# The way back of six groups of features by seven half products instead of eight, and two conversion steps of 24 weights on ScalarE

## The chip, the cores and the metric

The kernel runs on one core of a Trainium2 chip. The metric is the time of one execution in device microseconds; the time before is the median of three runs. A profile of one further execution gives the rows below. The engines are TensorE (PE, with its weight loads as PEld), VectorE (DVE), ScalarE (ACT), GpSimd (POOL) and the queue of SyncE (SP).

## The reference

Three parts, all in float32 as far as the result shows: linear attention with a normalization, a gated feed-forward layer, and a second feed-forward layer with an ELU.

```python
kv = np.einsum('bhsd,bhse->bhde', k, v)          # 4 batches, 8 heads, 576 tokens, 64 wide
out = np.einsum('bhsd,bhde->bhse', q, kv)
x = out / rms(out) * g_norm                       # then 2304 tokens x 512
xn = x / rms(x) * rms_g
g = xn @ w_gate                                   # 512 x 1536
x = (g * sigmoid(g) * (xn @ w_val)) @ w_out       # 1536 x 512
h = x @ w_in                                      # 512 x 2048
out = np.where(h > 0, h, np.exp(np.minimum(h, 0)) - 1) @ w_out2   # 2048 x 512
```

## The kernel before

The weights come as 64-bit floats. `conversion` makes 32-bit floats of a 128x512 tile of them in eight steps: `begin`, `scale`, `shift`, `sign`, `tail`, `add` on VectorE (four of them one-input steps of integers or floats, two with two inputs), then `part` on ScalarE and `rest` on VectorE, which split the value into a high part `h` and a low part `l` that TensorE takes as `fp32r`. Every product of the network is made of three such matmuls: high by high, high by low, low by high.

The 2304 tokens lie in five blocks of columns: block 0 with 256 and blocks 1 to 4 with 512. Blocks (1, 2) and (3, 4) are pairs. The hidden features come in chunks of 128: chunk `f` of the first layer has weights `g`, `v` (in) and `o` (back), 12 of them; the second layer has `i` and `p`, 16 of them. In this text "feature 8" is chunk 8. Two chunks make a group (`groups`), and the way back of a group adds up in PSUM over both chunks; the sum over groups is made in DRAM: ScalarE copies a bank to a buffer (`part`, five of them in the pools `P`), and GpSimd issues a DMA that adds it to `mid` (first layer) or `out` (second).

The hidden layer of a pair already goes by Strassen-Winograd's scheme from feature 2 or 4 on, and in all of the second layer (`paired`, named `('pu', layer, feature, first block)` in the rows): the products are made for halves of the model's width and of the pair's columns, seven instead of eight. The table `PRODUCTS` names for each one the bank (`a`, `b` or `c`), the half of the weight or sum of halves, and that of the input. Bank `a` takes the first, sixth, fifth and third product one on the other; ScalarE copies it after each of the first three (`snap`), and VectorE adds bank `b` or `c` to such a copy (`total`). Sums of weight halves are made by `weight_sums` (steps `w`, then `Sh` and `Sl` as their high and low part).

The way back is plain: `back` adds, for each block and each quarter `e` of the outputs, one step for each feature of the group, which is `back_part`: three matmuls of 512 columns (256 in block 0) onto bank `b`. `split_steps` makes the high and low part of an activation (`act`) on ScalarE and VectorE; then `dump` copies the bank.

What stands where on each engine is set by `Plan`: every step has an engine, a length, a rank and the steps and rooms it waits for; the planner takes the step that can start first, by rank where they tie, and writes the program in that order. Each engine then runs its list in order and waits on semaphores. `W` are 20 rooms for parts of weights, `A` those for parts of activations, `U` for intermediate values, `P` for copies on their way to DRAM.

Of the kernel before, what the change touches and what calls it, by code (L numbers as in the profile page):

```python
# [135 lines left out]
def linear_attention__swiglu__elu_kernel(
# [322 lines left out]
    def weight_sums(one, two, rank, users):  # L459

        def quarters():
            a, b = cw[one], cw[two]
# [107 lines left out]
    def split_steps(ph, f, t, erank, src, after, frees):  # L570
# [4 lines left out]
        def high():  # L575
            w = 2 * W if t else W
            a = res.tile([P, w], F32R, tag=plan.where[key], name=f"act{ph}_{f}_{t}")
            h = a[:, :n]
            acts[ph, f, t] = h, a[:, n:2 * n]
            nc.scalar.activation(h, src(), AF.Copy)  # L580
# [632 lines left out]
```

## Time and profile before

| | |
|---|---|
| median of 3 runs | 863.13 us (862.85 to 863.23) |
| profiled execution, its own time | 863.61 us |
| its span, first to last instruction | 861.6 us |
[...]
| TensorE busy | 849.0 us |
| VectorE busy | 641.4 us |
| ScalarE busy | 511.0 us |
| GpSimd busy | 232.8 us |

A busy time is the union of an engine's instructions; the last part of one can lie beside the start of the next, so distances between starts say more of an engine that never stops than durations do. Matmuls overlap most: they last 0.39 us and start 0.23 us apart. What lies around the span is 2.0 us.

### The profile page before, as it was taken

Reading aid. Unit: us, or ns where it says so; the run is one execution under the profiler, and the core shown is the slowest. Engines: PE = TensorE matmul, PEld = TensorE weight load, DVE = VectorE, ACT = ScalarE, POOL = GpSimd, SP = SyncE. Lnnn points to the kernel's source line nnn. Section 1 sums busy time; section 2 is a strip of 40 time slices with the busy share of each in tenths; the row PEclk is TensorE's granted clock in tenths of the full one; section 3 lists DMA queues with packets and bytes.
Section 4 is the critical chain, followed back from the end, with each engine's and each line's share of the span. In section 5 each row is a group of like instructions: output and inputs, shape, how many; then the busy total and the mean of one; then the engine's idle time right before and its main releaser. Section 6 shows DMA issues by size and latency. Waiting matters only on the chain.

```text
span 861.6 us, 12089 instructions
## 1 busy us (share of the span) xinstructions
PE 849.0 (99%) x4204; PEld 713.8 (83%) x4204; DVE 641.4 (74%) x1217; ACT 511.0 (59%) x979; POOL 232.8 (27%) x260
## 2 busy tenths in 40 slices
PE   7999999999999999999999999999999999999998
PEld 7988788888888888888888778888888888888886
DVE  6899899998736856675788999888675757674364
ACT  2788766445544545444544777777675767676652
POOL 2636523053033123113300000224233333423300
PEclk9999999999999999999999999999999999999999
DMA  9941479399076556727911254588788897868686
GB/s 366 364 154 43 117 157 179 92 181 201 28 121 118 111 106 119 142 69 128 220 50 61 74 184 154 129 175 155 148 154 163 145 153 133 170 110 121 124 230 210
DMA packets 57373, 126.14 MB, mean 146 GB/s; under 512 B 6496, under 2 KB 10080, under 8 KB 57312
## 3 DMA queue, kind: packets, MB, share of 16 engines
q0 software_dynamic: 29952, 51.92, 40.4%
q1 hardware_dynamic: 27360, 73.45, 24.3%
q8 instruction: 33, 0.54, 0.2%
q14 instruction: 28, 0.23, 0.1%
HBM read 59.28 MB, written 66.06 MB: 145 GB/s over the span
## 4 chain that ended last, share of the span: by engine, by line
PE 85%; DVE 7%; DMA 3%; ACT 2%; issue 1%; POOL 1%; SPq 0%; ACTq 0%; POOLq 0%; DVEq 0%
PE b L622 36%; PE hid_v L719 4%; PE hid_g L719 4%; PE hid_i L719 2%; PE po L298 1%; PE kv L262 1%; DMA wacc<-in_kv 1%; DMA wxl<-in_kv 1%; DVE xl L363 1%; POOL ri L318 1%; DVE far L693 1%; DVE act L584 1%; PE ('pu', 0, 9, 1)_a L529 1%; PE ('pu', 0, 11, 1)_a L529 1%; PE ('pu', 0, 4, 1)_a L529 1%
## 5 line engine op out<-in xcount | busy, mean ns | idle before, releaser
L657 ACT ACTIVATE part<-b 128x512 f32<-128x512 f32 (+1 forms) x246 | 138.8, 574 | 85.1 <-PE b L622 61.6
L663 POOL DMA_DIRECT2D out<-part x108 | 95.6, 893 | 304.8 <-ACT part L657 234.7
L622 PE MATMUL b<-act,h_p 128*128 128x512 f32 x512 | 158.5, 390 | 0.3 <-DVE act L584 0.2
L663 POOL DMA_DIRECT2D mid<-part x100 | 89.8, 995 | 234.7 <-ACT part L657 227.1
L622 PE MATMUL b<-act,h_o 128*128 128x512 f32 (+1 forms) x480 | 137.6, 370 | 3.0 <-DVE z L321 1.5
L622 PEld LDWEIGHTS b<-act,h_p 128*128 128x128 f32 x512 | 95.3, 188 | 21.1 <-DVE act L584 0.5
L622 PEld LDWEIGHTS b<-act,h_o 128*128 128x128 f32 x480 | 87.1, 188 | 21.7 <-DVE z L321 2.0
L622 PE MATMUL b<-act,l_p 128*128 128x512 f32 x256 | 99.6, 389 | 0.0
L622 PE MATMUL b<-act,l_o 128*128 128x512 f32 (+1 forms) x240 | 88.3, 368 | 0.0
L622 PEld LDWEIGHTS b<-act,l_p 128*128 128x128 f32 x256 | 48.1, 188 | 10.0
L622 PEld LDWEIGHTS b<-act,l_o 128*128 128x128 f32 x240 | 45.1, 188 | 7.6
L584 DVE TENSOR_TENSOR act<-e,act 128x512 fp32r<-128x512 f32 (+1 forms) x80 | 49.6, 631 | 1.5 <-ACT act L580 1.2
L580 ACT ACTIVATE act<-e 128x512 fp32r<-128x512 f32 (+1 forms) x80 | 45.9, 582 | 4.0 <-DVE e L763 3.8
L760 ACT ACTIVATE e<-e 128x512 f32<-128x512 f32 (+1 forms) x80 | 45.9, 583 | 0.8
L318 POOL TENSOR_TENSOR ri<-ms,nhalf 128x8 f32<-128x8 f32 x18 | 34.4, 1937 | 13.7 <-DVE ms L314 13.7
L719 PE MATMUL hid_g<-xh,h_g 128*128 128x256 f32 (+1 forms) x96 | 32.8, 342 | 0.0
L719 PE MATMUL hid_v<-xh,h_v 128*128 128x256 f32 (+1 forms) x96 | 32.5, 339 | 0.0
L719 PE MATMUL hid_g<-xl,h_g 128*128 128x256 f32 (+1 forms) x96 | 32.3, 337 | 0.0
L719 PE MATMUL hid_v<-xh,l_v 128*128 128x256 f32 (+1 forms) x96 | 32.3, 336 | 0.0
L719 PE MATMUL hid_g<-xh,l_g 128*128 128x256 f32 (+1 forms) x96 | 32.3, 336 | 0.0
L719 PE MATMUL hid_v<-xl,h_v 128*128 128x256 f32 (+1 forms) x96 | 32.3, 336 | 0.0
L693 DVE TENSOR_TENSOR far<-far,b 128x512 f32<-128x512 f32 (+1 forms) x38 | 24.3, 653 | 8.3 <-PE b L622 8.3
(1596 smaller groups left out, 2127.3 us busy)
## 6 DMA issues: line engine op xcount, KB each, us to landing
out<-part POOLq DMA_DIRECT2D x108, 256.0 KB, 5.4
mid<-part POOLq DMA_DIRECT2D x80, 256.0 KB, 6.3
raw_i<-in_w_in SPq DMA_DIRECT2D x16, 512.0 KB, 4.3
raw_p<-in_w_out SPq DMA_DIRECT2D x16, 512.0 KB, 4.7
raw_g<-in_w_gate SPq DMA_DIRECT2D x12, 512.0 KB, 5.5
raw_v<-in_w_val SPq DMA_DIRECT2D x12, 512.0 KB, 5.3
raw_o<-in_w_out SPq DMA_DIRECT2D x12, 512.0 KB, 6.9
out<-part SPq DMA_DIRECT2D x18, 256.0 KB, 2.5
```

Of the source, the lines that this page charges most:

```text
L262: nc.tensor.matmul(kv_acc[b][:, p, :], in_sb[i][r0:r1, p * P:(p + 1) * P], in_sb[i][r0:r1, DM + p * P:DM + (p + 1) * P], start=(i == tiles ...
L298: nc.tensor.matmul(po[r:r1, p * P:(p + 1) * P], qt[:, p, r:r1], kv_sb[b][:, p, :], start=True, stop=True)
L318: nc.gpsimd.tensor_tensor(ri, ms_t.pop(i), nhalf, op=ALU.pow)
L529: nc.tensor.matmul(pbank[unit, b], l[:, sl], r, start=first and c == 0 and i == 0, stop=c == 1 and i == 2, skip_group_check=True,)
L580: nc.scalar.activation(h, src(), AF.Copy)
L584: nc.vector.tensor_tensor(l, src(), h.bitcast(F32), op=ALU.subtract)
L622: nc.tensor.matmul(po, l, r, start=f == fs[0] and i == 0, stop=f == fs[-1] and i == 2)
L657: nc.scalar.activation(x, pbank["b", k, t, e][:, :n], AF.Copy)
L663: nc.gpsimd.dma_start(out=where(ph, t, e), in_=live.pop(key), accum_op=ALU.add)
L693: nc.vector.tensor_tensor(x, x, pbank["b", k, t, e][:, :n], op=ALU.add)
L719: nc.tensor.matmul(pbank[key], l, r, start=c == 0 and i == 0, stop=c == KD - 1 and i == 2)
L760: nc.scalar.activation(live[key], live[key], AF.Exp, scale=-1.0)
```

## The change

For six groups, features 4 to 9 of the first layer and groups 4, 8 and 12 (chunks 4 and 5, 8 and 9, 12 and 13) of the second, the way back of the two pairs goes by seven half products too (`back_halved`, `('pb', group, first block)` in the rows). Block 0 of these groups stays plain. The two chunks of the group are the two halves of the sum; the output weights' two halves and the pair's two blocks are the other two. The steps of a pair: high and low parts of three of the four activations and of four differences that are made in place over the activations (`split`, `less`: seven splits, four differences), 14 products of three matmuls on six banks (`a`, `b`, `c` for each of two column halves), eight copies by ScalarE straight into the `part` buffers, and six totals on VectorE. `weight_sums` makes the sums of the output weights' halves (`Sh_o`, `Sl_o`, `Sh_p`, `Sl_p`). An activation of such a group is no longer split by `split_steps`.

For the 24 weights `g`, `v`, `o` of features 4 to 11, `begin` and `tail` become ScalarE's: `Abs` with the scale 2^-112, and `Copy` with scale and bias; `scale` on VectorE keeps the minimum alone. The rooms of `act` are 12 single ones instead of 6 double ones, four of them also free for `U`. For a halved group both `o` are loaded after all `g` and `v`. In the last group of the first layer, block 0's products wait for the first pair's last ones, and the second pair's for block 0's.

```diff
+BACK_HALVED = [(0, 4), (0, 6), (0, 8), (1, 4), (1, 8), (1, 12)]
+SPARE = [f"{x}{f}" for f in range(4, 12) for x in "gvo"]
...
-        "U0": ["t0", "t1", "t2"], "C0": ["t3", "y0", "ad5"], "A0": AD[:3], "P0": P3[:2] + AD[3:5],
+        "U0": ["t0", "t1", "t2"], "C0": ["t3", "y0", "ad11"], "A0": AD[:6], "P0": P3[:2] + AD[6:8],
...
-        "A": AD, "A1": ["y0", "t3"], "P": P3 + K2, "U": Z4 + ["t2"], "C": ["t0", "t1", "t2"],
+        "A": AD, "A1": ["y0", "t3"], "P": P3 + K2, "U": Z4 + ["t2"] + AD[:7:-1], "C": ["t0", "t1", "t2"],
...
-            nc.vector.tensor_scalar(t["c"], t["high"], 0x7FFFFFFF, None, op0=ALU.bitwise_and)
+            if spare:
+                nc.scalar.activation(t["c"].bitcast(F32), t["high"].bitcast(F32), AF.Abs, scale=2.0**-112)
+            else:
+                nc.vector.tensor_scalar(t["c"], t["high"], 0x7FFFFFFF, None, op0=ALU.bitwise_and)
...
+            if spare:
+                nc.vector.tensor_scalar(cf, cf, INF_FIELD, None, op0=ALU.min)
...
+            if spare:
+                nc.scalar.activation(t["c"], t["low"], AF.Copy, scale=2.0**-29, bias=2.0**23)
...
+        turns = {0: [("b", 0, fs[-1], t_, 3) for t_ in PAIRS[0]], PAIRS[1][0]: [("b", 0, fs[-1], 0, 3)], PAIRS[1][1]: [("b", 0, fs[-1], 0, 3)]} if last and ph == 0 else {}
+        if k in HALVED and t:
+            return
...
+        def split(j, x):
+
+            def high():
+                parts[j] = tuple(place((unit, "s", j, y), F32R) for y in range(2))
+                nc.scalar.activation(parts[j][0], raw(*x), AF.Copy)
+
+            def low():
+                nc.vector.tensor_tensor(parts[j][1], raw(*x), parts[j][0].bitcast(F32), op=ALU.subtract)
...
+        split(11, A11)
+        less(1, A12, A11, A11)
+        split(21, A21)
+        less(3, A22, A12, A12)
+        split(3, A12)
+        split(22, A22)
+        less(2, A22, A11, A22)
+        split(2, A22)
+        less(4, A21, A22, A21)
+        split(1, A11)
+        split(4, A21)
...
+        before = {6: "snap1", 5: "snap2", 3: "snap4", 4: "total4"}
...
+            for i, (l, r) in enumerate(((wh, mh), (wh, ml), (wl, mh))):
+                nc.tensor.matmul(pbank[key], l[:, sl], r, start=first and i == 0, stop=i == 2, skip_group_check=True)
+
+        for o, (m, b, a, x, first) in enumerate(PRODUCTS):
+            for c in range(2):
+                plan.add(
+                    (unit, m, c), "PE", 0.68, rank + o + 0.5 * c, lambda m=m, c=c: product(m, c),
+                    [(unit, "l", x), *wdeps[a]] + ([(unit, before[m], c)] if m in before else []),
+                    [("o", (unit, b, c))] if first else [],
+                )
...
+            for m, j in ((1, 1), (6, 2), (5, 4), (3, 0)):
+                plan.add((unit, f"snap{j}", c), "ACT", AP_, rank, lambda j=j, copy=copy: copy(j), [(unit, m, c)], [("P", keys[j])])
+            for j, b, m in ((1, "b", 2), (4, "c", 7), (2, "c", 4)):
+                plan.add((unit, f"total{j}", c), "DVE", EW, rank, lambda j=j, b=b, total=total: total(j, b), [(unit, f"snap{j}", c), (unit, m, c)])
...
+            if k in HALVED and X:
+                back_halved(k, X, r + 50)
+            elif ph == 0 and k == last_k(0) and X:
```

The order on TensorE, where the way back of features 8 and 9 begins for blocks 1 and 2. Before, its products follow the first ones of feature 9's hidden layer for blocks 3 and 4:

```order
L529 MATMUL ('pu', 0, 9, 3)_b<-xh_945,h_g_3343 128x512
L529 MATMUL ('pu', 0, 9, 3)_b<-xl_946,h_g_3343 128x512
L529 MATMUL ('pu', 0, 9, 3)_b<-xh_945,l_g_3353 128x512
L622 MATMUL b_2_0_3875<-act_8_2_3677,h_o_3404 128x512 x2
L622 MATMUL b_2_0_3875<-act_8_2_3677,l_o_3413 128x512
L622 MATMUL b_1_0_3881<-act_8_1_3664,h_o_3404 128x512 x2
L622 MATMUL b_1_0_3881<-act_8_1_3664,l_o_3413 128x512
L622 MATMUL b_1_0_3881<-act_9_1_3863,h_o_3583 128x512 x2
L622 MATMUL b_1_0_3881<-act_9_1_3863,l_o_3594 128x512
```

Now, at the fifth and third product of the same way back, where `a_3889` and `a_3897` are the two column halves of bank `a`:

```order
L909 MATMUL ('pb', 5, 1)_a_3889<-('pb', 5, 1)_s_0_4006,Sh_o_1_3828 128x512
L909 MATMUL ('pb', 5, 1)_a_3889<-('pb', 5, 1)_s_1_4007,Sh_o_1_3828 128x512
L909 MATMUL ('pb', 5, 1)_a_3889<-('pb', 5, 1)_s_0_4006,Sl_o_1_3837 128x512
L909 MATMUL ('pb', 5, 1)_a_3897<-('pb', 5, 1)_s_0_4006,Sh_o_1_3828 128x512
L909 MATMUL ('pb', 5, 1)_a_3897<-('pb', 5, 1)_s_1_4007,Sh_o_1_3828 128x512
L909 MATMUL ('pb', 5, 1)_a_3897<-('pb', 5, 1)_s_0_4006,Sl_o_1_3837 128x512
L547 MATMUL ('pu', 0, 9, 3)_c<-xh_1137,Sh_g_1_3638 128x512
L547 MATMUL ('pu', 0, 9, 3)_c<-xl_1138,Sh_g_1_3638 128x512
L547 MATMUL ('pu', 0, 9, 3)_c<-xh_1137,Sl_g_1_3646 128x512
L909 MATMUL ('pb', 5, 1)_a_3889<-('pb', 5, 1)_s_0_3947,Sh_o_1_3828 128x512
L909 MATMUL ('pb', 5, 1)_a_3889<-('pb', 5, 1)_s_1_3948,Sh_o_1_3828 128x512
L909 MATMUL ('pb', 5, 1)_a_3889<-('pb', 5, 1)_s_0_3947,Sl_o_1_3837 128x512
```

The plain products stood in one piece, 48 in a row; the half products are spread among those of the hidden layer, and two products stand here between one use of a bank and the next.

The order on VectorE, around the first total of feature 10's hidden layer for blocks 3 and 4, close to the end of the first layer. Before:

```order
L555 TENSOR_TENSOR ('pu', 0, 10, 1)_u_4114<-('pu', 0, 10, 1)_u_4114,('pu', 0, 10, 1)_c 128x512
L422 TENSOR_SCALAR c_i_4259<-raw_i_4156 128x512
L788 TENSOR_TENSOR ('pu', 0, 10, 1)_u_4114<-('pu', 0, 10, 1)_u_4114,('pu', 0, 10, 1)_u_4047 128x512
L739 TENSOR_TENSOR sa_0_4247<-sa_0_4247,hid_v_10_0_4240 128x256
L425 ISA w_i_4269<-w_i_4269,c_i_4259 128x1024
L788 TENSOR_TENSOR ('pu', 0, 10, 1)_u_4233<-('pu', 0, 10, 1)_u_4233,s_10_1_4293 128x512
L584 TENSOR_TENSOR act_10_1_4296<-('pu', 0, 10, 1)_u_4114,act_10_1_4296 128x512
L584 TENSOR_TENSOR act_10_0_4303<-sa_0_4247,act_10_0_4303 128x256
L584 TENSOR_TENSOR act_10_2_4309<-('pu', 0, 10, 1)_u_4233,act_10_2_4309 128x512
L555 TENSOR_TENSOR ('pu', 0, 10, 3)_u_4316<-('pu', 0, 10, 3)_u_4316,('pu', 0, 10, 3)_b 128x512
```

Now:

```order
L763 TENSOR_TENSOR sa_0_4339<-sa_0_4339,hid_v_10_0_4335 128x256
L603 TENSOR_TENSOR act_10_1_1_4392<-('pu', 0, 10, 1)_u_4229,act_10_1_0_4391 128x512
L603 TENSOR_TENSOR act_10_0_0_4397<-sa_0_4339,act_10_0_0_4397 128x256
L928 TENSOR_TENSOR part_4_2_4403<-part_4_2_4403,('pb', 5, 3)_c_4347 128x512
L928 TENSOR_TENSOR part_3_2_4363<-part_3_2_4363,('pb', 5, 3)_c_4347 128x512
L496 SCALAR_TENSOR_TENSOR Sl_g_1_4427<-w_v_4277,Sh_g_1_4375 128x512
L496 SCALAR_TENSOR_TENSOR Sl_g_0_4435<-w_g_4206,Sh_g_0_4377 128x512
L928 TENSOR_TENSOR part_4_3_4430<-part_4_3_4430,('pb', 5, 3)_c_4366 128x512
L424 SCALAR_TENSOR_TENSOR w_o_4443<-raw_o_4219,c_o_4311 128x512
L573 TENSOR_TENSOR ('pu', 0, 10, 3)_u_4406<-('pu', 0, 10, 3)_u_4406,('pu', 0, 10, 3)_b 128x512
L436 ISA w_o_4443<-w_o_4443,c_o_4311 128x1024
L928 TENSOR_TENSOR part_3_3_4388<-part_3_3_4388,('pb', 5, 3)_c_4366 128x512
```

The conversion of the second layer's `i` stood ahead of that total; now totals of group 5 (features 8 and 9, rows of `part` with `('pb', 5, 3)`) stand there, with steps of a weight `o` between them.

The order on ScalarE after the first snapshot of feature 9's hidden layer for blocks 3 and 4. Before, where `part` with `b` are copies of the plain way back:

```order
L551 ACTIVATE ('pu', 0, 9, 3)_u_3870<-('pu', 0, 9, 3)_a 128x512
L580 ACTIVATE act_9_0_3873<-sa_0_3820 128x256
L657 ACTIVATE part_1_0_3897<-b_1_0_3881 128x512
L657 ACTIVATE part_1_1_3911<-b_1_1_3893 128x512
L657 ACTIVATE part_1_2_3921<-b_1_2_3907 128x512
L657 ACTIVATE part_1_3_3930<-b_1_3_3917 128x512
L657 ACTIVATE part_2_0_3937<-b_2_0_3875 128x512
L657 ACTIVATE part_2_1_3964<-b_2_1_3932 128x512
L430 ACTIVATE h_g_3975<-w_g_3879 128x512
```

Now, after that unit's second snapshot, where `L408` and `L431` are the two conversion steps that came over, and `part` with `('pb', 5, 1)_a` are snapshots of bank `a`:

```order
L569 ACTIVATE ('pu', 0, 9, 3)_u_4027<-('pu', 0, 9, 3)_a 128x512
L924 ACTIVATE part_2_2_4034<-('pb', 5, 1)_a_3889 128x512
L431 ACTIVATE c_v_3882<-raw_v_3772 128x512
L441 ACTIVATE h_v_4052<-w_v_4032 128x512
L408 ACTIVATE c_o_4058<-raw_o_3862 128x512
L569 ACTIVATE ('pu', 0, 9, 3)_u_4082<-('pu', 0, 9, 3)_a 128x512
L491 ACTIVATE Sh_g_1_4091<-w_v_4032 128x512
L491 ACTIVATE Sh_g_0_4099<-w_g_3848 128x512
L811 ACTIVATE s_9_3_4108<-('pu', 0, 9, 3)_a 128x512
L431 ACTIVATE c_o_4058<-raw_o_3862 128x512
L924 ACTIVATE part_2_3_4132<-('pb', 5, 1)_a_3897 128x512
```

Conversion steps and parts of weights now stand ahead of snapshots in the same list.

## Rows read from the trace of the kernel before

**Rows 1.** The page's head: span, and busy us of each engine (share).

```profile
span 861.6 us, 12089 instructions
...
PE 849.0 (99%) x4204; PEld 713.8 (83%) x4204; DVE 641.4 (74%) x1217; ACT 511.0 (59%) x979; POOL 232.8 (27%) x260
```

**Rows 2.** Windows: stretch, length, busy us of engines (instructions), clock, DMA share, GB/s.

```profile
core 0: us, PE busy (x) PEld busy (x) DVE busy (x) ACT busy (x) POOL busy (x), PEclk, DMA share, GB/s
0.00:200.00 200.00, 193.04 (x1111) 166.69 (x1112) 177.70 (x351) 125.08 (x259) 79.03 (x87) 1.00 0.66 183
...
120.00:220.00 100.00, 99.92 (x484) 83.61 (x483) 91.76 (x178) 54.24 (x100) 27.06 (x30) 1.00 0.77 163
...
200.00:400.00 200.00, 199.96 (x979) 168.67 (x978) 130.46 (x247) 95.32 (x178) 49.05 (x56) 1.00 0.59 113
...
400.00:440.00 40.00, 40.00 (x191) 33.59 (x190) 31.63 (x61) 20.35 (x39) 9.11 (x10) 1.00 0.65 147
440.00:540.00 100.00, 98.39 (x464) 80.41 (x463) 92.34 (x171) 65.03 (x120) 0.00 (x0) 1.00 0.35 116
...
540.00:780.00 240.00, 240.00 (x1118) 200.79 (x1117) 171.43 (x330) 165.79 (x314) 79.97 (x90) 1.00 0.79 146
```

**Rows 3.** Waits: engine, line, waited for, us in total, times, longest.

```profile
PE b L622 <- DVE z L321: 1.5, 1, 1.5
...
PE ('pu', 1, 0, 1)_a L529 <- ACT ('pu', 1, 0, 1)_u L551: 0.3, 1, 0.3
...
DVE Sl_i L483 <- PE b L622: 26.2, 5, 5.7
```

**Rows 4.** Timeline of TensorE, way back of features 8 and 9: start, us, what.

```profile
379.77 0.62 PE L622 MATMUL b<-act,h_o 128*128 128x512 f32 x2
...
390.43 0.39 PE L622 MATMUL b<-act,l_o 128*128 128x512 f32 x1
390.65 0.40 PE L622 MATMUL b<-act,h_o 128*128 128x256 f32 x2
```

**Rows 5.** Timeline of VectorE at 118 us, and at 443 us.

```profile
118.25 0.68 DVE L839 TENSOR_TENSOR T<-wx,T 128x512 fp32r<-128x512 f32 x1
118.85 0.41 DVE L422 TENSOR_SCALAR c_g<-raw_g 128x512 uint32<-128x512 uint32 x1
119.19 0.68 DVE L832 TENSOR_TENSOR wx<-wx,wx 128x512 f32<-128x512 f32 x1
...
443.03 0.69 DVE L555 TENSOR_TENSOR ('pu', 0, 11, 1)_u<-('pu', 0, 11, 1)_u,('pu', 0, 11, 1)_c 128x512 f32<-128x512 f32 x1 [0.19 <-ACT ('pu', 0, 11, 1)_u L551]
...
444.09 0.43 DVE L409 TENSOR_SCALAR c_p<-c_p 128x512 f32<-128x512 f32 x1
444.55 0.43 DVE L412 TENSOR_SCALAR c_p<-c_p 128x512 uint32<-128x512 uint32 x1
```

**Rows 6.** Groups of instructions by line and form: busy us, mean ns of one.

```profile
L584 DVE TENSOR_TENSOR act<-e,act 128x512 fp32r<-128x512 f32 x64 | 43.4, 684 | 1.1 <-ACT act L580 0.7
...
L555 DVE TENSOR_TENSOR ('pu', 1, 6, 3)_u<-('pu', 1, 6, 3)_u,('pu', 1, 6, 3)_c 128x512 f32<-128x512 f32 x2 | 1.4, 684 | 9.9 <-ACT ('pu', 1, 6, 3)_u L551 9.9
...
L405 DVE TENSOR_SCALAR c_g<-raw_g 128x512 uint32<-128x512 uint32 x12 | 5.2, 430 | 4.8 <-DMA raw_g<-in_w_gate 4.7
...
L430 ACT ACTIVATE h_p<-w_p 128x512 fp32r<-128x512 f32 x16 | 9.9, 625 | 0.3 <-PE ('pu', 0, 11, 3)_b L529 0.2
```

**Rows 7.** Timeline of ScalarE at 687 us.

```profile
686.77 0.59 ACT L657 ACTIVATE part<-b 128x512 f32<-128x512 f32 x1
687.25 0.63 ACT L580 ACTIVATE act<-e 128x512 fp32r<-128x512 f32 x1
687.77 0.60 ACT L551 ACTIVATE ('pu', 1, 8, 3)_u<-('pu', 1, 8, 3)_a 128x512 f32<-128x512 f32 x1
```

**Rows 8.** ScalarE's wait for a `part` buffer; and DMA issues, median us to landing.

```profile
ACT part L657 <- DMA out<-part: 17.1, 11, 3.5
...
out<-part POOLq DMA_DIRECT2D x108, 256.0 KB, 5.4
mid<-part POOLq DMA_DIRECT2D x80, 256.0 KB, 6.3
```

More of the change, by code (lines that the diff above doesn't have):

```diff
@@ L490, in weight_sums @@
         for x in (1, 0):
-            plan.add(("S", one, "h", x), "ACT", AS, rank + 0.5, lambda x=x: high(x), [("S", one, 3 - 2 * x + x)], [("W", ("Sh", one, x))])
+            plan.add(("S", one, "h", x), "ACT", AS, rank + 0.5, lambda x=x: high(x), [("S", one, 2 + x if across else 3 - x)], [("W", ("Sh", one, x))])
             plan.add(("S", one, "l", x), "DVE", EW, rank + 0.6, lambda x=x: low(x), [("S", one, "h", x)], [("W", ("Sl", one, x))])
@@ L501, in A, with A_back @@
         return S[one, int(j in (1, 3))], HALF * (j in (1, 4))
+    def A_back(one, two, j):
+        if j in (11, 12, 22):
+            return ready[one if j == 11 else two], HALF * (j == 22)
+        return S[one, int(j in (1, 4))], HALF * (j in (1, 3))
     T = {}
@@ L575, in high @@
         def high():
[L576 to L580, printed above, removed]
+            if t:
+                acts[ph, f, t] = tuple(place((*key, x), F32R) for x in range(2))
+            else:
+                a = place((*key, 0), F32R)
+                acts[ph, f, t] = a[:, :n], a[:, n:2 * n]
+            nc.scalar.activation(acts[ph, f, t][0], src(), AF.Copy)
         def low():
@@ L586, in split_steps @@
         kind = "A0" if ph == 0 and f < LONE else "A" if t else "A1"
-        plan.add(("ah", ph, f, t), "ACT", act_len(n, False), erank, high, after, [(kind, key)])
+        keys = [(*key, x) for x in range(2 if t else 1)]
+        plan.add(("ah", ph, f, t), "ACT", act_len(n, False), erank, high, after, [(kind, part) for part in keys])
         plan.add(("al", ph, f, t), "DVE", dve(n), erank, low, [("ah", ph, f, t)])
@@ L590, in split_steps @@
             plan.frees(x, [("al", ph, f, t)])
-        plan.frees(key, [(x, ph, f, t, e) for x, e in back_names(ph, f, t)])
+        for part in keys:
+            plan.frees(part, [(x, ph, f, t, e) for x, e in back_names(ph, f, t)])
     LONE, G = 2, 2
@@ L599, in linear_attention__swiglu__elu_kernel @@
     group_of = {(ph, f): k for k, (ph, fs) in enumerate(groups) for f in fs}
-    wname = {(0, "o"): "o", (1, "o"): "p"}
+    HALVED = [k for k, (ph, fs) in enumerate(groups) if (ph, fs[0]) in BACK_HALVED]
     def back_names(ph, f, t):
@@ L769, in elu_steps @@
             plan.frees(x, [("elu", f, t)])
+        if t and group_of[1, f] in HALVED:
+            return
         split_steps(1, f, t, erank, lambda: live[key], [("elu", f, t)], [key])
@@ L865, in linear_attention__swiglu__elu_kernel @@
     early_w = [n for n in LOADS if n in weight]
-    for f in range(LONE, F1):
-        LOADS += [f"g{f}", f"v{f}", f"o{f}"]
+    for f in range(LONE, F1, G):
+        fs = range(f, f + G)
+        if (0, f) in BACK_HALVED:
+            LOADS += [f"{x}{j}" for j in fs for x in "gv"] + [f"o{j}" for j in fs]
+        else:
+            LOADS += [f"{x}{j}" for j in fs for x in "gvo"]
     for f in range(0, F2, G):
@@ L966, in weight_users @@
             ph = int(kind == "p")
+            k = group_of[ph, f]
+            if k in HALVED:
+                ms = (1,) if f == groups[k][1][0] else (2, 4)
+                return [("b", ph, f, 0, e) for _, e in back_names(ph, f, 0)] + [(("pb", k, X[0]), m, c) for X in PAIRS for m in ms for c in range(2)]
             return [("b", ph, f, t, e) for t in range(len(blocks)) for _, e in back_names(ph, f, t)]
@@ L1012, in linear_attention__swiglu__elu_kernel @@
             weight_sums(f"i{f - 1}", n, rank + 5, sum_users(1, f - 1))
+        elif kind in "op" and group_of[ph, f] in HALVED and f % G:
+            k = group_of[ph, f]
+            weight_sums(f"{kind}{f - 1}", n, rank + 5, [[(("pb", k, X[0]), m, c) for X in PAIRS for m in ms for c in range(2)] for ms in ((6, 7), (3, 5))], True)
     for f in range(LONE):
```

83 lines of the change are left out of this document (74 added, 9 removed).

## Prediction

> **What bounds the kernel now.** I read the page first. TensorE is busy for 849.0 of the 861.6 us span; the next engine, VectorE, for 641.4, ScalarE for 511.0 [rows 1]. A busy share is an average, so the windows come second: from 200 to 440 us, where the first feed-forward runs on features 4 to 11, TensorE lacks 0.04 us, and from 540 to 780 us, in the second feed-forward, nothing at all; in between, at the change from one to the other (440 to 540 us), it lacks 1.6 us [rows 2]. [...] The list of TensorE's waits agrees: its longest, 1.5 us on `z`, comes early, while the attention part still runs [rows 3]. So where the change works, time goes where TensorE's instructions go, and the others count only if they make it wait. VectorE is the one to watch: 65% busy from 200 to 400 us, but 92% from 440 to 540 us, and 71% from 540 to 780 us [rows 2].
>
> **What goes away.** Per group and pair of blocks, 48 products of 512 columns (4 quarters of the outputs, 2 blocks, 2 features, 3 terms each) become 42 (7 half products, 2 column halves, 3 terms). Six groups and two pairs make 72 fewer, and the order of the changed program has just that many fewer on TensorE. The price of one is the distance between starts, not its duration, since they overlap: the way back of features 8 and 9 for the pair (1, 2) starts at 379.77 us, and behind the last of its 48 a 256-column one starts at 390.65 us, so 10.88 / 48 = 0.2267 us each [rows 4]. 72 x 0.2267 = **16.3 us** off TensorE, half in each feed-forward.
>
> **What is added on VectorE.** From the starts in its timeline, a 512-column instruction with two inputs takes a slot of 0.60 us and a conversion step 0.34; one that needs the result just before it, 0.46 instead of 0.34 [rows 5]. Per pair the old way has 4 low halves; the new one has 7, 4 differences and 6 totals: 13 more, 7.8 us. Per group two pairs give 15.6, and the sums of the output weights 4 half-width steps and 2 low halves, 4 x 0.34 + 2 x 0.60 = 2.6: 18.2 us a group, 109 us for six. The 24 weights give two steps each to ScalarE: 48 x 0.34 = 16.3 us less. Net +93 us, so about 734 of 845 us: no bound as a whole.
>
> The totals read PSUM. The trace has 684 ns for such a total (`u` with `_c`) and 684 ns for a low half that reads SBUF alone [rows 6], so I add nothing for PSUM. [...]
>
> By stage it is closer. From 200 to 440 us VectorE is busy for 130.5 + 31.6 = 162.1 us [rows 2]; three groups add 54.6, and of the 24 weights about 18 are converted there, 18 x 0.68 = 12.2 less: 204.5 in 240 - 36 x 0.2267 = 231.8 us, **88%**. From 540 to 780 us it is 171.4 + 54.6 = 226.0 in 231.8 us, **97%**, with none of the 24 weights. That is an upper bound, because busy time counts the last 0.08 us of an instruction, which the next one may overlap (0.68 long, 0.60 apart [rows 5]): with slots, 171.4 x 0.60 / 0.68 + 54.6 = 205.8, **89%**.
>
> How much TensorE loses at such shares only the nearest rows can say. From 120 to 220 us VectorE is 92% busy and TensorE lacks 0.08 us; from 440 to 540 us it is 92% too and TensorE lacks 1.6, because there each product waits for a fresh sum [rows 2]. Second feed-forward: between 0 (first row's rate) and 1.6% of 232 = 3.7 us (second row's); I take 1.0, nearer to the first, since the next feature's hidden products stand between the new ones, as the order rows of TensorE show. Transition: the order rows of VectorE in the section on the change have totals of group 5 (features 8 and 9) among feature 10's work, with splits that come with them some 8 instructions, 4.8 us, that the old way had behind it there; against them stand the 12 steps that features 10 and 11 hand to ScalarE, 4.1 us. Between 0 and 4.8 us; I take 1.0, as the two nearly cancel but 92% leaves little room.
>
> **What is added on ScalarE.** Per pair 3 more high halves, per group 2 for the weights: 8 x 0.52 = 4.2 us a group by its slots (0.48 from PSUM, 0.52 from SBUF [rows 7]), plus 48 x 0.52 = 25 us for the conversions: 511 + 50 of 845 us. The eight copies out of PSUM are as many as before. From 540 to 780 us: 165.8 + 12.5 = 178 of 231.8 us, 77%. Hidden, unless a copy is late.
>
> **The wait that changes its meaning.** A product on a bank now has to wait until ScalarE has copied what the bank held so far (`snap` before the sixth, fifth and third product). The copy goes into one of five buffers, and a buffer is held until its accumulating DMA has landed: 5.4 us for `out`, 6.3 for `mid` after the issue [rows 8]. Before, ScalarE waited 11 times for that, 17.1 us in all, longest 3.5 [rows 8], and TensorE lost nothing, since only the bank was kept. Now the same wait in ScalarE's queue holds up the high halves, `exp` and snapshots behind it, and through a snapshot TensorE. DMA and GpSimd get the same 96 accumulations as before, so the number of landings is unchanged, but the second snapshot keeps its buffer through four more products. Cost: 0 if the products put between hide it; 17.1 us if all of it came through. The order has 72 places where a half product takes up a bank again (24 banks, three times each): at 17 of them two products of 3 x 0.2267 = 0.68 us lie between, 1.36 us, at all others more, up to 15. A copy takes 0.60 us [rows 7]. The hidden layer's half products have the same least distance, and there TensorE's longest wait for a snapshot is 0.3 us, once [rows 3]. I take **0.5**.
>
> **Sum.** 863.6 us (this execution: 861.6 span and 2.0 around it) - 16.3 + 1.0 + 1.0 + 0.5 = 849.8; the execution is 0.5 above the median of the runs, so **849.3 us** against 863.1. The other edits (rooms for halves of `act` as tiles of their own, the order of loads, the order of the last group's blocks) move no work; each is hidden by the full TensorE, and is in the range with 1 us either way.
>
> **Rivals.**
> - *VectorE becomes the bound of the second feed-forward.* For it: 97% by busy time, some 12 dependent steps a group at 0.12 us more each (+4.3 us for three: 230 of 232), and waits of 26.2 us in five for TensorE to free a weight room (`Sl_i`) [rows 3], which VectorE could afford before. Against it: 89% by slots, and its order leaves other work ready. If a third of those waits stays uncovered, +8: 857 us, between 853 and 862.
> - *The snapshots wait for buffers; this one ends slower.* 12 pairs with two column halves are 24 chains; if each exposes one wait of 1.55 us, that is +37: 863.1 - 16.3 + 37 = 884 us. It decides from 16.3 / 24 = 0.68 us a chain on. Against it: the spacing above.
> - *Conversions on ScalarE come too late.* A step of 0.52 there replaces one of 0.34, twice, and each weight crosses engines more often, some 0.8 us more for each (two times 0.19, and two hand-overs that I put at 0.2 each, the nearest row being a total that waits 0.19 us for its copy [rows 5]). All exposed, 24 x 0.8 = 19 us: 868; a half, 858. Against it: weights are prepared one group ahead. [...]
> - *The new order also closes old gaps.* 1.6 us at the transition and 7.0 in the first 200 us [rows 2] are lost now; if 3 of them go and nothing is added, 844 to 846 us.
>
> **How the numbers follow.** Forecast, up to 6 us of new waits (846.8 to 852.8): 0.72. VectorE as bound: 0.14. Buffers: 0.04. Late conversions: 0.03, of them 0.01 beyond 863. Old gaps closed: 0.07. The range 845.5 to 856 leaves out the upper half of VectorE's case, the two slow ones and a little of the last: about 0.15. About 0.2% (1.7 us) is what a measurement of this kernel can tell from no change; faster by more 0.94, within it 0.02, slower 0.04.
>
> **What would show it.** Right: TensorE with 72 fewer products of 512 columns and still over 99% busy from 200 to 440 and from 530 to 765 us; VectorE near 735 us busy; no wait of TensorE for `part`, `s` or a DMA over 1 us. Wrong: a window of the second feed-forward where VectorE is over 95% busy and TensorE under 98% (first rival); ScalarE's `part` waiting for a DMA right ahead of a TensorE gap (second); TensorE waiting for `h_o` or `Sl_g` of features 4 to 11 (third). Slots on VectorE above 0.60 us for the new totals would make my price for it wrong.

## The result, and the profile after

The changed kernel takes **851.1 us** (median of four runs, 849.5 to 852.9) beside 863.0 for the kernel before on the same chip: a ratio of 0.9861, 95% interval 0.9848 to 0.9875. A second measurement on another chip, below, gave 0.9856. The forecast was 849.3, its range 845.5 to 856.

The profiled execution took 849.68 us. The head of its page, which answers to [rows 1]:

```profile
span 847.9 us, 12162 instructions
...
PE 833.1 (98%) x4132; PEld 699.7 (83%) x4132; DVE 729.8 (86%) x1361; ACT 558.8 (66%) x1075; POOL 237.8 (28%) x260
```

TensorE has 72 matmuls fewer, VectorE 88.4 us more (93 forecast), ScalarE 47.8 more (50). By windows, of the changed kernel (columns as in [rows 2]):

```profile
40.00:120.00 80.00, 75.98 (x435) 64.13 (x435) 75.08 (x153) 59.88 (x134) 44.03 (x33) 1.00 0.44 117
200.00:400.00 200.00, 200.00 (x978) 168.17 (x977) 163.91 (x299) 125.61 (x234) 48.03 (x55) 1.00 0.59 110
400.00:440.00 40.00, 40.00 (x200) 33.89 (x199) 36.57 (x69) 25.12 (x49) 10.69 (x12) 1.00 0.88 183
440.00:520.00 80.00, 78.16 (x365) 64.28 (x364) 78.44 (x148) 54.31 (x98) 0.00 (x0) 1.00 0.31 102
530.00:765.00 235.00, 234.76 (x1094) 195.22 (x1093) 208.08 (x391) 173.16 (x330) 80.25 (x90) 1.00 0.82 154
600.00:720.00 120.00, 120.00 (x561) 99.75 (x560) 110.95 (x207) 90.37 (x174) 44.46 (x51) 1.00 0.88 158
```

and three windows of the kernel before, which are not in the rows above:

```profile
40.00:120.00 80.00, 77.76 (x446) 66.55 (x445) 75.51 (x151) 60.70 (x135) 39.51 (x34) 1.00 0.41 108
440.00:520.00 80.00, 78.39 (x368) 63.57 (x367) 74.44 (x138) 50.33 (x93) 0.00 (x0) 1.00 0.31 100
600.00:720.00 120.00, 120.00 (x556) 100.10 (x555) 78.05 (x149) 80.52 (x151) 42.39 (x48) 1.00 0.82 150
```

Where the halved groups run TensorE stays full: those of the first layer lie between 200 and 440 us; in the second layer group 4 is at 577 to 629 us, group 8 at 667 to 715, and group 12 at 759 to 806, where TensorE is busy for 47.00 of 47 us. VectorE is now 92% busy from 600 to 720 us. What got worse is a stretch that the change was not about: from 40 to 120 us TensorE lacks 4.0 us in place of 2.2. TensorE's two longest waits, in the list of the changed kernel, are there too (at 104 and 52 us); the third row shown is at the transition, 488 us:

```profile
PE pt L355 <- ACT part L681: 2.0, 1, 2.0
PE pt L355 <- ACT z L341: 1.3, 1, 1.3
...
PE ('pu', 1, 0, 3)_a L547 <- DVE e L787: 1.1, 1, 1.1
```

Busy time hides small losses, so the table below counts **lost time**: the distances between the starts of neighbouring matmuls, less 0.2267, 0.1195 or 0.112 us for one of 512, 256 or 128 columns (their spacing in the trace of the kernel before), added up over a stretch of the profiled execution. Time at a lower granted clock counts as lost too. Each kernel was timed beside the kernel before on the same chip, so kernels are compared by their ratio to it; the lost time is that of one profiled execution, which need not be the median one. (The expectations of e6, e9, e11 and e13 were written with columns told from durations, which counts 1.1 us less from 40 to 120 us and 0.2 less from 440 to 520.)

| kernel | median us | ratio (95%) | products of 512 against before | lost 40-120 | lost 440-520 | lost 520-765 | lost in all |
|---|---|---|---|---|---|---|---|
| before | 863.0 | 1 | 0 | 3.5 | 4.2 | 0.7 | 19.1 |
| changed | 851.1 | 0.9861 (0.9848-0.9875) | -72 | 5.9 | 3.2 | 1.8 | 21.7 |
| e1 first layer halved only | 858.0 | 0.9928 (0.9914-0.9942) | -36 | 7.3 | 3.2 | 0.7 | 22.5 |
| e2 second layer only | 861.6 | 0.9975 (0.9965-0.9985) | -36 | 7.5 | 6.6 | 2.0 | 26.6 |
| e3 nothing halved or moved | 869.0 | 1.0057 (1.0042-1.0072) | 0 | 5.8 | 6.6 | 0.8 | 23.1 |
| e4 conversion on VectorE | 857.1 | 0.9919 (0.9906-0.9933) | -72 | 7.3 | 8.6 | 1.8 | 29.4 |
| e5 changed, again | 850.6 | 0.9856 (0.9843-0.9870) | -72 | 5.8 | 3.2 | 1.7 | 22.5 |
| e6 sums in old rooms | 851.7 | 0.9866 (0.9851-0.9881) | -72 | 3.5 | 7.4 | 1.4 | 23.6 |
| e7 a fourth group | 853.6 | 0.9889 (0.9876-0.9903) | -84 | 7.3 | 3.2 | 7.2 | 29.6 |
| e8 six groups | 860.5 | 0.9969 (0.9959-0.9980) | -108 | 7.3 | 3.2 | 15.0 | 43.1 |
| e9 all i, p on ScalarE | 852.2 | 0.9873 (0.9858-0.9888) | -72 | 5.9 | 5.4 | 1.6 | 24.3 |
| e10 three buffers | 1001.7 | 1.1605 (1.1581-1.1629) | -72 | 6.0 | 13.5 | 33.6 | 171.5 |
| e11 e7, late i, p on ScalarE | 850.6 | 0.9841 (0.9828-0.9855) | -84 | 7.3 | 3.2 | 3.0 | 25.3 |
| e13 e11, first pair's sums in old rooms | 848.2 | 0.9827 (0.9813-0.9840) | -84 | 3.9 | 3.2 | 4.4 | 23.0 |

### The profile page after: what moved, and what is told of

It is laid out like the page before. It is cut to its first block, busy times and chain, and to the rows that moved or that the text cites. A ratio compares the mean times of both kernels' runs of the same rounds, so it can differ in the third digit from the quotient of the medians.

```text
span 847.9 us, 12162 instructions
## 1 busy us (share of the span) xinstructions
PE 833.1 (98%) x4132; PEld 699.7 (83%) x4132; DVE 729.8 (86%) x1361; ACT 558.8 (66%) x1075; POOL 237.8 (28%) x260
## 4 chain that ended last, share of the span: by engine, by line
PE 80%; DVE 10%; DMA 4%; POOL 2%; ACT 2%; issue 1%; SPq 0%; DVEq 0%; POOLq 0%; ACTq 0%
PE b L643 19%; PE hid_v L743 4%; PE hid_g L743 4%; PE hid_i L743 2%; PE po L300 1%; POOL ri L338 1%; PE kv L264 1%; DMA wacc<-in_kv 1%; DVE act L603 1%; DVE far L717 1%; DMA wxl<-in_kv 1%; DMA raw_i<-in_w_in 1%; DVE xl L1296 1%; POOL ri L320 1%; DVE far L965 1%
## 5 line engine op out<-in xcount | busy, mean ns | idle before, releaser
L643 PE MATMUL b<-act,h_p 128*128 128x512 f32 x320 | 99.3, 390 | 1.0 <-ACT act L599 0.5
L681 ACT ACTIVATE part<-b 128x512 f32<-128x512 f32 (+1 forms) x150 | 81.6, 559 | 18.0 <-PE b L643 12.1
L643 PE MATMUL b<-act,h_o 128*128 128x512 f32 (+1 forms) x288 | 78.3, 358 | 1.5 <-DVE far L717 0.7
L643 PEld LDWEIGHTS b<-act,h_p 128*128 128x128 f32 x320 | 60.0, 188 | 14.5 <-DVE act L603 1.4
L643 PE MATMUL b<-act,l_p 128*128 128x512 f32 x160 | 62.3, 389 | 0.0
L643 PEld LDWEIGHTS b<-act,h_o 128*128 128x128 f32 x288 | 50.8, 189 | 12.6 <-DVE far L717 1.9
L643 PE MATMUL b<-act,l_o 128*128 128x512 f32 (+1 forms) x144 | 51.0, 354 | 0.0
L599 ACT ACTIVATE act<-e 128x512 fp32r<-128x512 f32 (+1 forms) x56 | 31.6, 568 | 7.9 <-DVE e L787 7.7
L643 PEld LDWEIGHTS b<-act,l_p 128*128 128x128 f32 x160 | 30.0, 188 | 6.2
L603 DVE TENSOR_TENSOR act<-e,act 128x512 fp32r<-128x512 f32 (+1 forms) x56 | 33.8, 610 | 0.3 <-ACT act L599 0.2
```

Of the source, the lines that this page charges most:

```text
L599: nc.scalar.activation(acts[ph, f, t][0], src(), AF.Copy)
L603: nc.vector.tensor_tensor(l, src(), h.bitcast(F32), op=ALU.subtract)
L643: nc.tensor.matmul(po, l, r, start=f == fs[0] and i == 0, stop=f == fs[-1] and i == 2)
L681: nc.scalar.activation(x, pbank["b", k, t, e][:, :n], AF.Copy)
```

## Experiments

**Which half of the change pays (e1, e2).** Edits:

```diff
-BACK_HALVED = [(0, 4), (0, 6), (0, 8), (1, 4), (1, 8), (1, 12)]
+BACK_HALVED = [(0, 4), (0, 6), (0, 8)]      # e1
+BACK_HALVED = [(1, 4), (1, 8), (1, 12)]     # e2
```

> Only features 4 to 9 of the first feed-forward go back by seven half products; the second layer's way back is plain, everything else as changed. Theory of the forecast (each product of 512 columns taken away is worth 0.2267 us, the rest is hidden): 36 fewer products, -8.2 us, and what the changed kernel loses in its first 120 us (some 2 us, since the order there is the same) stays: 856 to 857 us. Rival (VectorE is the bound of the second feed-forward): the halved groups of the second layer give back less than 8.2 us, so this kernel would lie within 5 us of the changed one, at 855 or less.

> Only groups 4, 8 and 12 of the second feed-forward go back by seven half products; the first layer's way back is plain. Theory of the forecast: -8.2 us, and 0 to 1 us for VectorE near its limit from 540 to 770 us: 855 to 857 us. Rival (VectorE bound): 858 to 862 us, with TensorE under 98% busy in a window of the second feed-forward. Rival (the first layer's halves cost something, by late conversions or snapshots): this kernel would be more than 4.1 us nearer to the changed one than the forecast says, at 854 or less.

e1 took 858.0 us, 1 above the 856 to 857 expected, but clearly not the rival's 855 or less; its profiled execution (858.65) has a fall of the granted clock (0.80 on the mean from 105 to 110 us) among its 7.3 us of early loss (last section). e2 missed: 861.6 us, too slow by some 5. Its second layer loses only 2.0 us; what is dear is the transition, 6.6 us in place of 3.2. So this was neither rival: the first layer's halved groups do not only save their 36 products, the transition behind them also loses 3.4 us less.

**What the moved rooms and turns cost alone (e3).** `BACK_HALVED = []` and `SPARE = []`; the single rooms, their lending to `U` and the order of the last group stay.

> No way back is halved and no conversion step goes to ScalarE; what stays of the change are the twelve single rooms for parts of activations, the rooms that they lend to intermediate values, and the order of the last group's blocks. Theory: these move no work, and the loss in the first 120 us comes from the new order that the rooms bring there: 863 to 865.5 us, with TensorE short of about 2 us more than before between 40 and 120 us. Rival (the early loss comes with the conversion steps on ScalarE or with the halved groups): 863 us as before, with the early windows as before. A gain from the rooms alone would show as less than 862.

869.0 us, above the 865.5 that I allowed: these edits make the kernel slower by 0.6%. The trace, of an execution of 867.3 us, has both places, +2.4 us from 40 to 120 us (as expected) and +2.4 at the transition (not expected). "They move no work" was true, and the order that they bring still costs.

**Conversion back on VectorE (e4).** `SPARE = []`, all six groups halved.

> All six groups halved, but the conversion steps of the 24 weights stay on VectorE: 48 steps of 0.34 us, +16.3 us there, most of it between 120 and 420 us. Theory (VectorE has room in the first feed-forward: 82% busy from 200 to 400 us as changed, 88 to 90% with these steps): TensorE loses 0 to 2 us, 850 to 853 us; the ScalarE part of the change is worth little. Rival (VectorE is what the first feed-forward hangs on, and ScalarE's help pays for the halving): 855 to 867 us, with TensorE waiting for sums or parts of weights between 120 and 440 us.

857.1 us: 5.3 us dearer by the ratios (0.9919 less 0.9858, the mean of the changed kernel's two, times 863), so the time is the rival's. But its place is wrong: from 200 to 440 us TensorE stays full, 240.00 of 240 us, with VectorE busy for 211.7. The transition loses 8.6 us in place of 3.2, a part of it at a lower clock, behind TensorE's longest wait there:

```profile
440.00:520.00 80.00, 75.74 (x347) 60.96 (x346) 77.31 (x146) 49.33 (x91) 0.00 (x0) 0.98 0.31 102
```

```profile
PE ('pu', 1, 0, 1)_a L547 <- ACT ('pu', 1, 0, 1)_u L569: 1.9, 1, 1.9
```

**Is VectorE what the transition hangs on (e9)?**

```diff
-SPARE = [f"{x}{f}" for f in range(4, 12) for x in "gvo"]
+SPARE = [f"{x}{f}" for f in range(4, 12) for x in "gvo"] + [f"{x}{f}" for f in range(16) for x in "ip"]
```

> The changed kernel, with two conversion steps of the second layer's 32 weights i and p on ScalarE as well: 64 steps of 0.34 us off VectorE, 64 of 0.52 on to ScalarE; 16 of them lie between 430 and 530 us, where VectorE is 97.7 of 100 us busy and TensorE loses 3.0 us between 440 and 520. Theory (VectorE is what the transition hangs on; the 24 weights paid because they gave it room there): TensorE loses 1 to 2 us in place of 3.0, VectorE is below 95% busy, 848 to 850 us. Rival (the transition hangs on the chain of snapshot, total and split itself, or on steps that come late by way of ScalarE): 851 to 856 us, with TensorE's loss there 3 us or more.

My theory is not borne out: VectorE has a little less to do there (77.6 of 80 us in place of 78.4) and TensorE loses more, 5.4 us. It is a weak test, since VectorE is still 97% busy, not under the 95% that I had expected:

```profile
440.00:520.00 80.00, 77.46 (x356) 62.41 (x355) 77.58 (x142) 59.58 (x109) 0.00 (x0) 1.00 0.35 113
```

In e2 and e3 VectorE is even less busy (75 of 80) and 6.6 us are lost. So the loss at the transition, between 3.2 and 8.6 us, does not follow VectorE's load. What is left is the order of the steps: e6, below, changes only the rooms of some sums and with them the order, and loses 7.4 us at nearly the changed kernel's load (78.8 us). Which pair of steps decides it stays open.

**The early gaps (e5, e6).** e5 is the changed kernel again, the measure for e6 to e8. e6 gives the sums their five old rooms:

```diff
-                        [("U", ("wx", t, k))],
+                        [("UX", ("wx", t, k))],     # "UX" is "U" without the four lent rooms
```

> The changed kernel once more, word for word, beside the kernels of this call: 849.5 to 853 us, lower where its mean clock is 1.00 and higher where it is below. [...]

> The changed kernel, but the sums of a pair's input halves (the steps that write wx and w3, VectorE, two inputs in SBUF) may use only the five rooms that they had before, not the four lent ones. This gives VectorE and GpSimd their old order in the first 120 us but for 14 of 180 VectorE rows. Theory (the lent rooms let VectorE run these steps without a break; GpSimd's ri, which took 3.52 us where it had taken 0.78, waits for a break in VectorE; ScalarE's z and TensorE's transposes wait for ri): ri is short again at 49 us, the gaps of 1.45 us at 52 us and 2.1 us at 104 us go, TensorE loses some 2.4 us between 40 and 120 us as before, and the kernel takes 1.5 to 3.5 us less than the changed one beside it. Rival (ri was long for another reason, such as the place of its code): the long ri and both gaps stay, and the time is the changed kernel's within 1 us.

The edit of e6 moves the steps that write `wx` alone; those of `w3`, which the expectation names too, keep all rooms. e5 came out as expected, 850.6 us; its trace has no fall of the clock at 104 us (1.00 from 100 to 120 us), so whether such falls part its runs stays open. In e6 the mechanism was right, the price of the whole was not. GpSimd's `ri` at 49 us, in the timeline of the kernel before, of the changed one and of e6 (start, length):

```profile
49.55 0.78 POOL L336 TENSOR_TENSOR ri<-ms,nhalf 128x1 f32<-128x1 f32 x1 [2.84 <-ACT junk L332]
```

```profile
49.35 3.52 POOL L338 TENSOR_TENSOR ri<-ms,nhalf 128x1 f32<-128x1 f32 x1 [2.85 <-ACT junk L334]
```

```profile
49.66 0.78 POOL L338 TENSOR_TENSOR ri<-ms,nhalf 128x1 f32<-128x1 f32 x1 [2.85 <-ACT junk L334]
```

In the kernel before, VectorE's steps there wait for each other's results, with breaks of 0.03 to 0.04 us between them:

```profile
49.51 0.42 DVE L412 TENSOR_SCALAR c_v<-c_v 128x512 uint32<-128x512 uint32 x1
49.96 0.69 DVE L416 SCALAR_TENSOR_TENSOR w_v<-raw_v,c_v 128x512 uint32<-128x512 uint32 x1
50.68 0.43 DVE L422 TENSOR_SCALAR c_v<-raw_v 128x512 uint32<-128x512 uint32 x1
51.15 0.69 DVE L425 CUSTOM_DVE_ANT_0 w_v<-w_v,c_v 128x1024 uint16<-128x1024 uint16 x1
```

In the changed kernel it runs on without a break:

```profile
49.31 0.42 DVE L420 TENSOR_SCALAR c_v<-c_v 128x512 uint32<-128x512 uint32 x1
49.64 0.68 DVE L1218 TENSOR_TENSOR wx<-xh,xl 128x512 f32<-128x512 f32 x1
50.24 0.68 DVE L424 SCALAR_TENSOR_TENSOR w_v<-raw_v,c_v 128x512 uint32<-128x512 uint32 x1
50.85 0.68 DVE L1218 TENSOR_TENSOR wx<-xh,xl 128x512 f32<-128x512 f32 x1
51.45 0.42 DVE L433 TENSOR_SCALAR c_v<-raw_v 128x512 uint32<-128x512 uint32 x1
51.78 0.68 DVE L1218 TENSOR_TENSOR wx<-xh,xl 128x512 f32<-128x512 f32 x1
52.39 0.69 DVE L763 TENSOR_TENSOR sa<-sa,hid_v 128x512 f32<-128x512 f32 x1
```

The `wx` sums fill what were breaks between dependent conversion steps. `ri` ends at 52.87, half a microsecond after `sa` began, the first of these that reads one of its inputs (`hid_v`) from PSUM. ScalarE's `z` waits for it, and TensorE's transposes for `z`:

```profile
52.91 0.72 ACT L341 ACTIVATE z<-z,ri 128x512 f32<-128x512 f32 x1 [2.72 <-POOL ri L338]
```

In e6 both gaps are gone and the early loss is 3.5 us as before. Yet the kernel is no faster (851.7 us beside 850.6), since the new order loses 7.4 us at the transition:

```profile
40.00:120.00 80.00, 77.76 (x447) 66.52 (x445) 75.50 (x152) 60.95 (x136) 39.58 (x34) 1.00 0.43 115
440.00:520.00 80.00, 76.54 (x344) 60.30 (x343) 78.80 (x147) 52.99 (x97) 0.00 (x0) 1.00 0.32 109
```

**How near VectorE's bound is (e7, e8, e11).** `(1, 6)` added to `BACK_HALVED`; for e8 all of `(1, 2)` to `(1, 12)`; e11 is e7 with `i` and `p` of chunks 4 to 15 in `SPARE`.

> One more group of the second feed-forward halved, chunks 6 and 7, so that chunks 4 to 9 follow each other. TensorE: 12 products fewer, -2.7 us. VectorE by slots: a halved group takes 43.4 us there (25.2 of a plain one and 18.2), TensorE 38.6, so three in a row are 14 us too much, less what VectorE is ahead. Theory (VectorE bounds a stretch of halved groups, and the plain ones between let it catch up): 850 to 862 us, with TensorE idle near the end of chunk 9. Rival (TensorE alone sets the end): 2.7 us less than the changed kernel, 848 to 849 us.

> Six groups of the second feed-forward halved, chunks 2 to 13. TensorE: 36 products fewer than the changed kernel, -8.2 us. VectorE by slots: six times 43.4 = 260 us against TensorE's 232. Theory (VectorE is the bound there): 860 to 872 us, VectorE over 97% busy from 530 to 770 us. Rival (TensorE alone): 843 us.

> The four groups of the run with chunks 6 and 7 added (chunks 4 to 9, 12 and 13 of the second layer), with two conversion steps of the weights i and p of chunks 4 to 15 on ScalarE: 48 steps of 0.34 = 16.3 us off VectorE between 530 and 770 us; the order up to the transition stays that of the changed kernel. Theory (the fourth group lost its gain because VectorE was 118 of 120 us busy from 600 to 720 us): with some 8 us less there TensorE loses under 1.5 us in that stretch in place of 5.8, 847.5 to 849.5 us, 1 to 3 us less than the changed kernel. Rival (the half products' own chain of snapshot and total, or the part buffers, cost it): no better than the four groups alone, 852 to 854 us.

The windows of e7, e8 and e11, one row each:

```profile
600.00:720.00 120.00, 117.22 (x537) 94.20 (x536) 117.97 (x222) 91.40 (x175) 40.83 (x47) 1.00 0.86 148
```

```profile
600.00:720.00 120.00, 113.84 (x518) 90.55 (x517) 119.73 (x229) 88.25 (x170) 41.09 (x46) 1.00 0.83 147
```

```profile
600.00:720.00 120.00, 119.51 (x554) 97.70 (x554) 116.99 (x212) 102.39 (x200) 42.23 (x49) 1.00 0.89 150
```

e7 came out in its range (850 to 862 us) and e8 at the low end of its own (860 to 872). With a fourth group VectorE is 98% busy, TensorE falls to 97.7% and does 24 matmuls fewer than the changed kernel in the same 120 us: 5.4 us lost for the 2.7 that the group saves. With six it is 99.8%. e11 gives VectorE less to do for each product, and TensorE is back at 554 matmuls; the kernel is 3.0 us faster than e7 (850.6 against 853.6, beside 863.5 and 863.1 of before). So VectorE is what a fourth group hangs on. The median is still 1 us above what I expected, and no better than the changed kernel's 851.1 and 850.6 with three groups: from 600 to 720 us e11 loses 2.4 us, more than the 1.5 that I gave it, and its trace has a fall of the clock in the early stretch (0.84 on the mean from 105 to 110 us, 0.82 from 110 to 115).

The 43.4 and 38.6 us of e7's expectation are both too low, since they share 240 us among six groups. In the kernel before, the hidden products of chunk 4 start at 562.7 us and those of chunk 12 at 748.7, so a plain group takes TensorE 46.5 us, a halved one 12 products fewer, 43.8. In e8, where VectorE does not pause, one halved group follows the other every 48.4 us (chunk 6 at 598.4, chunk 12 at 743.5). VectorE needs 4.6 us more for a halved group than TensorE, much as the expectation had it (4.8). Worked with 46.5 us to a group, the forecast's prices give VectorE 47.5 us for a halved one by slots (171.4 x 46.5 / 240 x 0.60 / 0.68 + 18.2) and 51.4 by busy time; the measured 48.4 is nearer to the slots.

**The buffers (e10).** `"P": P3` in place of `P3 + K2`.

> The changed kernel with three buffers for copies on their way to memory (those of the pool P) in place of five. Theory of the forecast (with five a snapshot hardly waits for a buffer): the price with five is about 0, and shows itself only with fewer. A buffer is held from the copy to the landing, about 8 us (0.6 of copy, 0.5 to 2 of totals, 5.6 to 5.9 to land), and a halved pair needs eight in some 19 us, so that 8 times 8 / 19 = 3.4 buffers are in use on the mean: with three TensorE must wait, 853 to 870 us, with ScalarE's part waiting for a DMA. Rival (buffers already cost time with five): TensorE's waits for snapshots grow from a visible amount; in the trace with five they would be over 0.5 us each. If nothing changes (850 to 852), the buffers are no limit even with three and my price of 8 us for one is too high.

1001.7 us, far beyond my 870. The list of ScalarE's waits has a part of the reason, copies that wait for a landing, 41.0 us in these rows:

```profile
ACT part L681 <- DMA out<-part: 15.7, 10, 3.0
ACT part L924 <- DMA out<-part: 13.1, 9, 3.7
ACT part L924 <- DMA mid<-part: 12.2, 3, 5.4
```

The order itself changes with the number of rooms, so the 151 us are not these waits alone; TensorE's lost 171.5 us include stretches at a granted clock of 0.50 (one from 436 to 446 us; the mean over the execution is 0.957). With four buffers (e12, expected at 852 to 880 us) there is no time: the planner came to a point where no step could start, so where between three and five the price begins stays open.

**Both losses out (e13).** e11, and `"UX"` for the sums of the pair (1, 2) only.

> The last run's kernel (four groups of the second layer halved, i and p of chunks 4 to 15 partly converted on ScalarE), and only the wx sums of the pair (1, 2) kept to the five old rooms. VectorE's first 180 rows are near those of before again, while TensorE's order at the transition is word for word that of the last run. Theory (VectorE's unbroken run of these sums holds GpSimd's ri back; where the old rooms cost time it was by another order at the transition): ri is short at 49 us, no gap of TensorE at 52 or 104 us but one of about 1.5 us at 99 us as before, TensorE's loss between 40 and 120 us 2 to 2.7 us in place of 4.7 to 5.7, at the transition 3.0 us as in the last run, and 846 to 848.5 us. Rival (the long ri, or the price at the transition, has another cause): 849 to 851 us, with one of the two losses unchanged.

848.2 us, the fastest of all: its interval (to 0.9840) ends below those of the changed kernel (from 0.9843 and 0.9848). `ri` at 49 us takes 0.78 again, and the two stretches are:

```profile
40.00:120.00 80.00, 77.73 (x444) 66.05 (x443) 74.88 (x151) 61.18 (x135) 40.36 (x34) 1.00 0.44 115
440.00:520.00 80.00, 78.15 (x365) 64.24 (x364) 78.44 (x147) 55.06 (x101) 0.00 (x0) 1.00 0.32 105
```

The transition is the changed kernel's (3.2 us lost) with the early order of before. That shows that the sums' rooms are the cause of the early loss, and that e6's loss at the transition does not come with its cure. Against e11 the intervals overlap: 3.4 us of early loss are gone, 1.4 of them the fall of the clock in e11's trace, and from 520 to 765 us e13 loses 1.4 more. The early loss of 3.9 us is 2.8 by the count of the expectation, which had 2.7 at most.

## Why the prediction was right, point by point

- **The products taken away, -16.3 us: right.** There are 72 fewer, and the median distance between starts of 512 columns is 0.227 us before and after. From TensorE's first start to its last it is 856.37 us before and 842.70 after: -13.67, which is -16.32 and 2.65 of lost time more (19.07 to 21.72).
- **Second feed-forward, +1.0: measured +1.2** (0.7 to 1.8 lost from 520 to 765 us), and 0.6 more behind 765 us. The size is about right, the working is not. It put three halved groups in the window from 540 to 780 us, but the third lies behind it: before, the way back of chunks 12 and 13 starts at 780.3 us for the pairs, and now it runs from 759 to 806. VectorE is busy for 208.1 of 235 us from 530 to 765, 89%, with two halved groups (171.4 + 2 x 18.2 = 207.8 by busy time). That the sum by slots for three groups gave 89% as well is luck; what speaks for slots is e8. The third group shows on VectorE in the last window, before and after:

```profile
780.00:861.60 81.60, 77.58 (x350) 63.63 (x349) 37.86 (x62) 39.41 (x75) 15.66 (x18) 1.00 0.72 174
```

```profile
765.00:847.90 82.90, 78.42 (x358) 64.20 (x356) 60.52 (x102) 44.15 (x87) 15.77 (x18) 1.00 0.74 172
```

  The new totals, which read PSUM, take 0.68 to 0.69 us, as the low halves that read SBUF alone do (686 ns), and start 0.60 apart, as priced.
- **Transition, +1.0: the step that failed in sign; -1.0 measured.** It went by VectorE's share of busy time, which rose from 74.4 to 78.4 of 80 us while TensorE lost less. e2, e3, e4 and e9 show that the share says little there; what is left is the order, and why this one lost less is not shown.
- **Snapshots waiting for buffers, +0.5: 0 measured.** The list does have a wait of TensorE for `part` of over 1 us, a sign against the forecast as it was written: 2.0 us. It lies at 104 us, where no group is halved and ScalarE itself had waited 2.87 us for `ri` (last section). No product of a halved group is in the list. ScalarE's waits for a buffer fell from 20.7 us to 5.5. With two buffers fewer the kernel is 151 us slower, so the rival was worth naming.
- **The other edits, "within 1 us either way": mis-sized.** They cost 2.4 us from 40 to 120 us. I had argued that TensorE is full, but that holds from 200 us on; before that, [rows 2] show 7 us lost and VectorE at 89%, so a room lent to a pool could change the order there.
- **The rivals.** VectorE as bound: not with three groups, but with the fourth, by the sign that was named for it (VectorE over 95%, TensorE under 98%). Late conversions: the opposite, the ScalarE steps and the order that came with them are worth 5.3 us, most of it at the transition. Old gaps closed: 1.0 at the transition, eaten by the early ones.
- **The sum** of new losses was forecast at 2.5 us and measured at 2.65, but that it fits so closely is luck: the early 2.4 us were put at nothing, the transition has the other sign, and the buffers cost nothing. The 16.3 us are what was understood. The profiled execution took 849.68 us, forecast 849.8; the median of the runs, 851.1, is 1.8 above its forecast.

## What to carry to other kernels

Count the bounding engine's instructions first: their number times their spacing, 16.3 us, gave the gain but for 2.65 us of new lost time. Then compare, group by group, the slots of the engine that gets the work with the time of the bounding one, and see in which window each group lies: here VectorE's 48.4 us for a halved group against TensorE's 43.8 could be carried only with a plain group between. And ask of every room that a change lends to a pool where else in the program the planner may use it, since the dearest effect, at 52 and 104 us, lay more than 100 us ahead of the first halved group.

## What the runs showed of the hardware

- **GpSimd waits for VectorE.** A power of 128x1 takes 0.5 to 1.1 us elsewhere in the traces of the kernel before and the changed one, and 3.52 and 4.40 us (at 49 and 100 us of the changed kernel) where VectorE's SBUF instructions follow each other without a break; it ends 0.4 to 0.5 us after the first break or PSUM read. `ri` waited through the six VectorE instructions at 49 us, with one SBUF input or two. By what means they hold it was not shown; that these VectorE steps are the cause e6 and e13 show, where it takes 0.78 us at 49 us. The second of the two, and ScalarE behind it:

```profile
99.97 4.40 POOL L338 TENSOR_TENSOR ri<-ms,nhalf 128x1 f32<-128x1 f32 x1 [0.57 <-ACT junk L334]
```

```profile
104.41 0.72 ACT L341 ACTIVATE z<-z,ri 128x512 f32<-128x512 f32 x1 [2.87 <-POOL ri L338]
```

- **A gap can cost twice.** In the traces of e1, e2, e4, e7, e8 and e11 the granted clock fell behind the 2.1 us gap at 104 us (0.73 to 0.93 on the mean of 5 us between 105 and 115 us); the windows of e7 have it at 0.50:

```profile
105.00:106.00 1.00, 0.00 (x0) 0.00 (x0) 0.00 (x0) 0.91 (x2) 0.88 (x2) 1.00 0.00 0
106.00:107.00 1.00, 0.13 (x1) 0.14 (x2) 0.64 (x2) 0.81 (x2) 0.00 (x0) 1.00 0.72 59
107.00:108.00 1.00, 1.00 (x6) 0.91 (x7) 1.00 (x4) 0.38 (x2) 0.00 (x0) 0.66 0.98 170
108.00:109.00 1.00, 1.00 (x4) 0.80 (x3) 1.00 (x3) 1.00 (x4) 0.00 (x0) 0.50 0.81 268
109.00:110.00 1.00, 1.00 (x4) 0.71 (x3) 1.00 (x3) 0.47 (x1) 0.00 (x0) 0.50 0.07 27
```

  The early loss is 7.3 to 7.5 us in these traces, and 5.8 to 6.0 in those with the same gap whose clock stayed at 1.00 there (changed, e3, e5, e9 and e10), so I put the fall at some 1.4 us. In e4 the clock fell once more, at 480 us (0.69 from 480 to 485), behind the wait of 1.9 us shown above. Neither trace of the changed kernel has the fall; its runs at 852.5 and 852.9 us have mean clocks of 0.996 and 0.993, those at 849.5 and 849.7 have 0.999 and 1.000, so falls probably part them, but where they lay is not shown. In the runs of e13 (847.5 to 848.8), where that gap is gone, every mean clock was 0.999 or more.
